# Attention values with queries on partitions: the turned P becomes the stationary operand, V the moving one, and the softmax factor is applied to x

## The chip, the cores and the metric

The kernel runs on one core of one Trainium2 chip. The metric is the device time in microseconds (us) of one execution of the whole program; lower is better. A core has five engines that run their own instruction streams side by side: TensorE (PE, with its weight loads shown apart as PEld), VectorE (DVE), ScalarE (ACT), GpSimd (POOL) and SyncE (SP, which here only issues DMA). Each stream is in program order, and semaphores tie them together.

## The reference

Two stages. First a windowed attention with a linear position bias over 8 batches, 8 heads, 576 positions and a head width of 64; a query sees itself and the 127 positions before it:

```python
scores = scale * (q @ k.T) + slope[h] * -(i - j)     # kept where 0 <= i - j < 128
attn = exp(scores - rowmax); attn /= attn.sum(-1) + 1e-9
x = (attn @ v)                                       # then (B, H, S, D) -> (4608, 512)
```

Then a "soft" mixture of experts over all 4608 tokens with 32 slots, 4 for each of 8 experts:

```python
logits = x @ phi                                     # 4608 x 32
d = softmax over tokens (axis 0); slot_input = d.T @ x
slot_out[e] = relu(slot_input[e] @ w1[e]) @ w2[e]    # 512 -> 1024 -> 512
c = softmax over slots (axis 1);  out = c @ slot_out
```

All arithmetic is float32.

## The kernel before, in words

**Tiles and groups.** A batch has 576 = 4 x 128 + 64 queries, so five query tiles t = 0 to 4, the last one (the tail) 64 wide. A group (b, t, g) is four heads of a full tile (g = 0 or 1), or all eight heads of a tail, two heads side by side in the 128 partitions. That makes 72 groups. One turn of the main loop (lines 770 to 797) handles several groups at different stages; each engine executes its share in the order written, since the whole kernel is scheduled by hand (`manual_schedule`).

**One group on its way.** `scores` (L227) puts the position bias (bf16, L248, or L236 for t = 0) and q k^T (L255, or L241) into one of two PSUM tiles `s4`, for t > 0 as 32-query strips with a key window of 160. On DVE, `merge` folds the window to 128 columns (L268, L270, L272), `rowmax` reduces it (L290) and `bias` scales the maximum (L293). On ACT, `expo` writes P = exp(...) of four heads to SBUF and sums its rows (L342). POOL adds the epsilon (`total`, L298), DVE inverts (L302), and `normalise` multiplies each of the four 128 x 128 blocks of P by its row's factor on DVE (L307). Three turns later PE transposes the four blocks (`flip`, L352), ACT copies them out of PSUM (`split`, L359), and POOL masks them into the part that belongs to the same key tile, `pd`, and the one that belongs to the key tile before, `pp` (L361, L363, for tails L366, L368). One turn after that, `values` multiplies:

```python
for ph in halves_of:                    # previous and own key tile
    for par in range(2):                # head of the pair -> PSUM partitions 0-63 or 64-127
        nc.tensor.matmul(
            xp[D * par:D * par + D, j, 0:w],
            lhsT=v_slot[b, t - 1 + ph][0:rows, D * h:D * h + D],     # stationary: V, 64 columns
            rhs=src[:, 2 * par + i] ...,                             # moving: P^T, 128 columns
            start=(ph == halves_of[0]), stop=(ph == halves_of[-1]))
```

(L388.) x comes out transposed, 128 feature rows of two heads by w queries. One such float32 matmul is two instructions in the trace, each with its own weight load. A group of t = 1 to 3 has 16 such loads and matmuls, one of t = 0 has 8 (no key tile before it), a tail has 32.

**After the values of a tile.** ACT copies x from PSUM (`x_store`, L404), PE transposes it back to tokens on partitions (`x_flip`, L409) and ACT copies that (`x_keep`, L418), because the mixture needs x both ways round: for the logits (`logits`, L427) and for the slot inputs (`slot_sum`, L510). The mixture's online softmax over tokens runs once for each batch, over the four full tiles as four "lanes" of 32 rows; the tails of two batches share a tile, which is handled behind every odd batch by further, narrow steps (`logits_tail` L438, small flips L468 and L496, `slot_tail` L517). The last batch is in the order 1, 2, 3, 4, 0 and has its own closing code (lines 799 to 880): two lanes, then a join with three more.

**The rest.** The main loop puts its PE work in the order flip, values, scores of the next group, then what `todo` holds under "pe" (x_flip, logits and so on). DMA is issued by SP in program order: q three groups ahead, K and V as their slots come free, and expert weights, 64 units of 512 KB, of which 36 go into a ring during attention and 11 into places (`place`) that attention has left. After attention come `hidden` (L911, first expert layer), `expert_out` (L947), `slot_stack` (L960), `slot_inputs` before it (L661, the only place besides `slot_stack` where a full 128 x 128 float32 block that isn't being transposed is the stationary operand), and `combine` (L968, L974, output DMA L976).

Of the kernel before, what the change touches and what calls it, by code (L numbers as in the profile page):

```python
# [10 lines left out]
F32 = mybir.dt.float32  # L11
# [10 lines left out]
DM = H * D  # L22
# [20 lines left out]
EAGER = 2  # L43
FLAG = 3
LAG = 4
FINAL = (3, 4, 0)
# [8 lines left out]


def width(t):
    return P if t < 4 else TAIL
# [10 lines left out]
def tile_attn_softmoe(  # L69
# [26 lines left out]
    fine = cpool.tile([P, 14], F32, name="fine")  # L96
    low, m_run, s_run = fine[:, 0:1], fine[:, 1:3], fine[:, 3:4]
    comb = cpool.tile([P, NS], F32, name="comb")
    mix = cpool.tile([P, NS], F32, name="mix")
# [7 lines left out]
    area = cpool.tile([P, 19, HW], F32, name="area")  # L107

    kall = kq[:, 0:NB * P].rearrange("p (n j w) -> p n j w", n=NB, j=NPAIR)
    qs = [kq[:, NB * P + 2 * P * i:NB * P + 2 * P * i + 2 * P] for i in range(3)]  # L110
    half = [slice(64 * par, 64 * par + 64) for par in range(2)]

    def halves(i):
        return area[:, i].rearrange("p (u w) -> p u w", u=4)

    xts = [halves(i) for i in (0, 1, 12, 13)]
    xt_t = halves(17)
    p4s = [halves(i) for i in (2, 3, 18)]
    pas, pps = [halves(i) for i in (6, 8, 7)], [halves(i) for i in (7, 9)]
    vs = [area[:, i] for i in (11, 5, 10)]  # L120
    xns = [area[:, i] for i in (16, 4, 14, 15)]
# [3 lines left out]
    areas = {i: area[:, i:i + 2].rearrange("p a w -> p (a w)") for i in range(0, 18, 2)}  # L125
    place = [ks[1], areas[14], ks[0], ks[2]] + [areas[i] for i in (0, 10, 6, 4, 16, 12, 8)]
# [16 lines left out]
    def order(b):  # L143
        return (1, 2, 3, 4, 0) if b == last else range(NT)

    def pos(b, t):
        return order(b).index(t)

    def lane(b, t):
        return (t - 1) % 4 if b == last else t  # L150

    groups = [(b, t, g) for b in range(B) for t in order(b) for g in range(2 if t < 4 else 1)]
    number = {key: i for i, key in enumerate(groups)}
    n = len(groups)
    v_loads = [(b, t) for b in range(B) for t in range(NT)]
    fin = slice(3 * NS, P)
# [7 lines left out]
    def load_q(i, eng=None):  # L164
        b, t, g = groups[i]
        o = 4 * P * t + 2 * P * g
        (eng or nc.sync).dma_start(qs[i % 3], qd[b, :, o:o + 2 * P])
# [4 lines left out]

    v_slot = {}

    def load_v(again=False):
        if again:
            b, t, v_slot[last, 0] = last, 0, area[:, 13]
        else:
            b, t = v_loads[len(v_taken)]
            v_slot[b, t] = vs[len(v_taken) % 3]  # L180
            v_taken.append((b, t))
        nc.sync.dma_start(v_slot[b, t][0:width(t)], vd[b, P * t:P * t + width(t)])

    def load_v_pair():
        new = [len(v_taken), len(v_taken) + 1]
        for i in new:
            v_slot[v_loads[i]] = vs[i % 3]
            v_taken.append(v_loads[i])
        for o in (0, DM // 2):
            for i in new:  # L190
                b, t = v_loads[i]
                nc.sync.dma_start(
                    v_slot[b, t][:, o:o + DM // 2], vd[b, P * t:P * t + P, o:o + DM // 2])
# [3 lines left out]
    with tc.manual_schedule(engines=ORDERED):  # L197
        warm = area[:, 2].bitcast(BF16)[:, 0:512]
# [4 lines left out]
        nc.vector.memset(fine[:, 10:11], -1.0)  # L203
# [11 lines left out]
        for i in range(WARM):  # L215
            nc.tensor.matmul(free[i % 4], lhsT=warm[:, 0:P], rhs=warm, start=True, stop=True)
        nc.gpsimd.memset(lg, LOW)
        nc.gpsimd.memset(area[:, 3, 0:P], 1.0)
        nc.gpsimd.affine_select(
            unit_r, area[:, 3, 0:P], [[1, P]], ALU.is_equal, 0.0, base=0, channel_multiplier=-1)  # L220
        load_v()
        nc.scalar.dma_start(cst[:, P:], cstd)
        nc.scalar.dma_start(phi, phid)
        for t in range(2, NT):
            load_k(0, t)

    def scores(i):  # L227
        b, t, g = groups[i]
        s4 = s4s[i % 2]
# [867 lines left out]
```

## Time and profile before

| | us |
|---|---|
| three runs | 290.46, 290.97, 292.67; median 290.97 |
| span of the profiled execution (first to last instruction) | 289.1 |
| median of the runs less that span | 1.9 |
| first merge on DVE to last merge (attention loop) | 5.4 to 219.1 |
| last merge to the first matmul of `hidden` | 219.1 to 235.7 |
| `hidden` to the end | 235.7 to 289.1 |

In the profile, a row of a timeline reads: start in us, length in us, engine, line, operation, output<-inputs, shape, xcount, and in brackets the idle time ahead with what ended it. In a shape, "128*64 128x64" means an array tile of 128 rows by 64 columns and operands of 128 partitions by 64 elements. For a weight load the second number of the array tile is the number of columns that are loaded. In the list of groups the number behind the bar is busy time in us, the mean of one in ns, then the engine's idle time ahead of the group and what ended most of it.

### The profile page before, as it was taken

What the parts mean: (1) busy time and instruction counts of PE and PEld (TensorE: products, weight loads), DVE (VectorE), ACT (ScalarE), POOL (GpSimd) and SP (SyncE); (2) the same over time, 40 slices, a digit from 0 to 9 for tenths busy, and PEclk for the clock granted to TensorE, in tenths of its full rate; (3) what the DMA queues carried; (4) which work ended last, traced back from release to release, by engine and by line L of the source; (5) the groups of instructions that cost most, each with busy time, mean ns of one, the idle gap of its engine ahead of it and who ended that gap; (6) DMA issues with size and microseconds to landing.
All of it is one profiled execution on the core that took longest, in us unless ns stands there. A gap on an engine that the chain in (4) does not pass through costs nothing.

```text
span 289.1 us, 13085 instructions
## 1 busy us (share of the span) xinstructions
PE 272.9 (94%) x5164; PEld 191.0 (66%) x5164; DVE 233.3 (81%) x729; ACT 204.5 (71%) x811; POOL 92.7 (32%) x206
## 2 busy tenths in 40 slices
PE   7499999999999999999999999999899999999983
PEld 3367777777677767776777677767676753476641
DVE  3899999999989999988999999979989443234452
ACT  2788888978988978978798887978797241023351
POOL 2025515442444354235324550634455001000000
PEclk9799999999999999999999999999999999999995
DMA  6645278868786887867678869675547789999897
GB/s 193 223 131 169 81 228 266 261 201 284 212 265 201 287 279 242 246 231 247 216 249 258 282 199 291 218 252 173 185 158 238 231 285 311 417 417 398 352 378 285
DMA packets 35025, 72.58 MB, mean 251 GB/s; under 512 B 4210, under 2 KB 15124, under 8 KB 34964
## 3 DMA queue, kind: packets, MB, share of 16 engines
q1 hardware_dynamic: 34244, 71.24, 74.0%
q8 instruction: 41, 0.67, 0.9%
q10 hardware_dynamic: 720, 0.51, 0.6%
q14 instruction: 20, 0.16, 0.1%
HBM read 62.29 MB, written 9.44 MB: 248 GB/s over the span
## 4 chain that ended last, share of the span: by engine, by line
PE 47%; DVE 44%; ACT 3%; issue 3%; POOL 1%; ACTq 0%; DVEq 0%; POOLq 0%
DVE area L307 16%; DVE s L290 11%; PE xp L388 8%; DVE s L270 6%; PE op L947 5%; PE hp L911 5%; PE po L968 4%; PE pt L352 4%; PE s L255 4%; DVE s L268 3%; PE xq L409 2%; PE lp L427 2%; ACT area L342 2%; PE s L248 2%; PE ap L510 1%
## 5 line engine op out<-in xcount | busy, mean ns | idle before, releaser
L342 ACT ACTIVATE area<-s,nb 128x128 f32<-128x128 f32 x288 | 102.5, 374 | 21.5 <-DVE nb L293 20.2
L307 DVE TENSOR_SCALAR area<-area,rs 128x128 f32<-128x128 f32 x286 | 79.2, 338 | 0.6 <-DVE nb L293 0.3
L388 PE MATMUL xp<-area 128*64 128x128 f32 (+1 forms) x1104 | 75.2, 271 | 2.2 <-POOL area L361 1.3
L388 PEld LDWEIGHTS xp<-area 128*64 128x64 f32 x1104 | 56.2, 136 | 17.4 <-issue 8.7
L342 ACT ACTIVATION_READ_ACCUMULATOR area<-s,nb 128x1 f32 x288 | 60.8, 211 | 0.0
L290 DVE TENSOR_REDUCE s<-s 128x4 f32<-128x512 f32 x71 | 49.5, 698 | 2.2
L359 ACT COPY area<-pt 128x512 f32<-128x512 f32 x70 | 42.0, 600 | 11.0 <-PE pt L352 10.8
L298 POOL TENSOR_SCALAR rs<-sm 128x4 f32<-128x4 f32 x70 | 13.8, 197 | 99.7 <-ACT area L342 98.9
L352 PE MATMUL pt<-unit_r,area 128*128 128x128 f32 x284 | 45.6, 282 | 0.0
L255 PE MATMUL s<-kq 64*32 64x160 f32 x1792 | 42.0, 302 | 0.3 <-DMA kq<-k_t 0.3
L352 PEld LDWEIGHTS pt<-unit_r,area 128*128 128x128 f32 x284 | 31.9, 142 | 14.2 <-PE s L255 5.0
L361 POOL TENSOR_SCALAR_AFFINE_SELECT area<-area 128x512 f32<-128x512 f32 x48 | 31.6, 658 | 25.8 <-ACT area L359 24.5
L270 DVE COPY_PREDICATED s<-cst,s 128x512 f32<-128x512 int32 x48 | 32.9, 686 | 0.7 <-PE s L255 0.5
L363 POOL TENSOR_SCALAR_AFFINE_SELECT area<-area 128x512 f32<-128x512 f32 x48 | 31.4, 655 | 3.3
L255 PEld LDWEIGHTS s<-kq 64*32 64x32 f32 x1792 | 29.6, 107 | 1.0 <-DMA kq<-q_t 0.5
L248 PE MATMUL s<-ramp,ones 64*32 64x320 bf16 x448 | 18.7, 310 | 5.0 <-ACT area L342 4.8
L974 DVE COPY ob<-po 128x384 f32<-128x384 f32 x24 | 12.5, 554 | 13.5 <-PE po L968 11.8
L409 PE MATMUL xq<-unit_r,area 128*128 128x128 f32 x136 | 22.0, 284 | 0.5
L404 ACT COPY area<-xp 128x512 f32<-128x512 f32 (+1 forms) x37 | 20.9, 565 | 2.0 <-PE xp L388 1.6
L418 ACT COPY area<-xq 128x512 f32<-128x512 f32 x34 | 20.8, 611 | 0.0
L974 ACT COPY ob<-po 128x384 f32<-128x384 f32 x24 | 10.5, 482 | 13.7 <-PE po L968 13.7
L409 PEld LDWEIGHTS xq<-unit_r,area 128*128 128x128 f32 x136 | 14.5, 141 | 6.4 <-issue 3.2
(167 smaller groups left out, 309.8 us busy)
## 6 DMA issues: line engine op xcount, KB each, us to landing
w<-w SPq DMA_DIRECT2D x53, 512.0 KB, 5.1
out<-ob SPq DMA_DIRECT2D x24, 384.0 KB, 4.2
kq<-q_t SPq DMA_DIRECT2D x69, 128.0 KB, 3.2
kq<-k_t SPq DMA_DIRECT2D x32, 256.0 KB, 3.7
area<-v_n SPq DMA_DIRECT2D x31, 256.0 KB, 4.3
area<-w SPq DMA_DIRECT2D x8, 512.0 KB, 5.0
area<-v_n SPq DMA_DIRECT2D x12, 128.0 KB, 3.4
kq<-w SPq DMA_DIRECT2D x3, 512.0 KB, 6.3
```

The costliest lines, as they stand in the source:

```text
L248: nc.tensor.matmul(s4[32 * c:32 * c + 32, 2 * par:2 * par + 2, 32 * r:32 * r + WIN], lhsT=ones[rows, 0:32], rhs=ramp[rows, h], start=True, ...
L255: nc.tensor.matmul(s4[32 * c:32 * c + 32, 2 * par + jj, 32 * r:32 * r + WIN], lhsT=qt[rows, 2 * h + jj if t == 4 else jj, 32 * r:32 * r + 32],
L270: nc.vector.copy_predicated(s4[:, :, P:2 * P], bc(mask_u, 1, 4), s4[:, :, 0:P])
L290: nc.vector.tensor_reduce(st[key]["mx"][:, us], merged(key, us), axis=AX.X, op=ALU.max, negate=True)
L307: mul(p4[:, u], p4[:, u], st[key]["rs"][:, u:u + 1])
L342: nc.scalar.activation(s["p4"][:, u], merged(key, u), AF.Exp, bias=s["nb"][:, u:u + 1], scale=SCALE, accum_out=s["sm"][:, u:u + 1],)
L352: nc.tensor.transpose(s["pt"][:, u], s["p4"][:, u], ident)
L359: copy(pa[:, us], s["pt"][:, us])
L361: nc.gpsimd.affine_select(pp[:, us], pa[:, us], [[0, m], [-1, P]], ALU.is_gt, 0.0, base=0, channel_multiplier=1)
L363: nc.gpsimd.affine_select(pa[:, us], pa[:, us], [[0, m], [1, P]], ALU.is_ge, 0.0, base=0, channel_multiplier=-1)
L388: nc.tensor.matmul(xp[D * par:D * par + D, j, 0:w], lhsT=v_slot[b, t - 1 + ph][0:rows, D * h:D * h + D], rhs=src[:, 2 * par + i] if t < 4 ...
L409: nc.tensor.transpose(xq[:, P * j:P * j + P], x_of(b, t)[:, j], ident)
```

## The change

- `values`: P^T is the stationary operand (all 128 queries as columns, lines `pp`, `pd`), V moves, 64 columns for a head, and x comes out with queries on partitions. The counts stay 16 (t = 1 to 3) and 8 (t = 0) loads and matmuls a group.
- The tails of an even batch and the next odd one form one tile of 128 queries, which is handled with the odd batch in two groups like any other; its matmuls take 64 columns of P^T at a time and go to PSUM partitions 0-63 and 64-127. The key tile of the tail is padded with zeros to 128 rows (`v4_even`, `v4_odd`), so that both parts use all 128 rows. There are still 72 groups, now 36 tiles of two.
- `normalise` is gone. `x_store` on DVE multiplies x on its way out of PSUM by the factor of its query and head, one 128 x 512 instruction for a tile. `total` (POOL) and `inverse` (DVE) run once for a tile rather than once for a group.
- `x_store` gives the token layout, so `x_flip` makes the transposed one; `x_keep` copies that. Their number is 36, one for each tile. `x_flip` stands ahead of `flip` in the next turn.
- The mixture handles nine sets of four tiles, all alike; the narrow steps for tails and the join of the last batch are gone. The last set is in the closing code, with three lanes and then the fourth.
- P is turned two turns after its scores rather than three (`FLAG`), and its values come after three rather than four (`LAG`).
- SBUF: V in four slots rather than three, extra slots for the tails' K and V, six rows of x rather than four, 15 places for early weights rather than 11. On the host, q is laid out anew. The call that builds the program gets `dynamic_dma_scratch_size=64`.

The core of the diff:

```diff
-FLAG = 3
-LAG = 4
+FLAG = 2
+LAG = 3
+NXN = 6
+NQ = NTT // 4
...
-    place = [ks[1], areas[14], ks[0], ks[2]] + [areas[i] for i in (0, 10, 6, 4, 16, 12, 8)]
+    place = [ks[1], ks[0], ks[2]] + [areas[i] for i in (0, 14, 2, 4, 10, 8, 12, 6, 20, 22, 16, 18)]
...
-        return (1, 2, 3, 4, 0) if b == last else range(NT)
...
-    groups = [(b, t, g) for b in range(B) for t in order(b) for g in range(2 if t < 4 else 1)]
+        return (1, 2, 3, 4, 0) if b == last else range(4 + b % 2)
+
+    tiles = [(b, t) for b in range(B) for t in order(b)]
+    groups = [(b, t, g) for b, t in tiles for g in range(2)]
...
+    def load_k_even(b):
+        nc.sync.dma_start(kt, kd[b, :, 3 * 4 * P:NB * P])
...
+    def load_v_tails(b):
+        nc.sync.dma_start(v3_even, vd[b, 3 * P:4 * P])
+        nc.sync.dma_start(v4_even[0:TAIL], vd[b, 4 * P:S])
+        nc.sync.dma_start(v4_odd[0:TAIL], vd[b + 1, 4 * P:S])
...
-    def normalise(key, us, mul=nc.vector.tensor_scalar_mul):
-        p4 = st[key]["p4"]
-        for u in range(4)[us]:
-            mul(p4[:, u], p4[:, u], st[key]["rs"][:, u:u + 1])
+    def total(k):
+        st["rs", k] = work.tile([P, H], F32, tag="rs", name="rs")
+        nc.gpsimd.tensor_scalar(st["rs", k], st.pop(("sm", k)), EPS, 1.0, op0=ALU.add, op1=ALU.mult)
+
+    def inverse(k):
+        nc.vector.reciprocal(st["rs", k], st["rs", k])
...
+    def softmax_front(i):
+        new = groups[i]
         merge(new)
+        rowmax(new, ALL)
+        bias(new, ALL)
         filler()
         filler()
+        if i % 2 and i > 1:
+            inverse((i - 3) // 2)
...
+        for jj in range(2):
+            for par in range(2):
+                u, h = 2 * par + jj, 4 * g + 2 * jj + par
+                cols = slice(D * h, D * h + D)
+                for ph in (1,) if t == 0 else (0, 1):
+                    src = (pp, pd)[ph][:, u]
+                    if t < 4:
+                        nc.tensor.matmul(
+                            xp[:, cols], lhsT=src, rhs=v_slot[b, t - 1 + ph][:, cols],
+                            start=(ph == 0 or t == 0), stop=(ph == 1))
+                    else:
+                        for rows, v in zip(half, ((v3_even, v_slot[b, 3]), (v4_even, v4_odd))[ph]):
+                            nc.tensor.matmul(
+                                xp[rows, cols], lhsT=src[:, rows], rhs=v[:, cols],
+                                start=(ph == 0), stop=(ph == 1))
+
+    def x_store(k, hs=slice(0, H)):
+        cols = slice(D * hs.start, D * hs.stop)
+        nc.vector.tensor_tensor(
+            xns[k % NXN][:, cols].rearrange("p (h d) -> p h d", d=D),
+            st["x", k][:, cols].rearrange("p (h d) -> p h d", d=D),
+            bc(st["rs", k][:, hs], 2, D), op=ALU.mult)
...
+        x_store(k)
+        do("flip", i + 1, x_flip, k)
+        do("act", i + 1, x_keep, k)
+        if k % 4 == 3:
+            do("pe", i + 1, logits, q)
...
-                softmax_front(new, groups[i - 1])
+                softmax_front(i)
...
+            if i and i % 2 == 0:
+                total(i // 2 - 1)
+            run("flip", i)
             if i >= FLAG:
                 flip(groups[i - FLAG])
                 split(groups[i - FLAG])
             run("act", i)
             if i >= LAG:
                 values(groups[i - LAG])
-                after_values(i, groups[i - LAG])
             if i + 1 < n:
                 scores(i + 1)
+            if i >= LAG:
+                after_values(i, groups[i - LAG])
...
-    nc = bacc.Bacc("TRN2", target_bir_lowering=False, num_devices=1)
+    nc = bacc.Bacc("TRN2", target_bir_lowering=False, num_devices=1, dynamic_dma_scratch_size=64)
```

More of the change, by code (lines that the diff above doesn't have):

```diff
@@ new lines, in x_store, with x_flip @@
+    def x_store(k, hs=slice(0, H)):
[4 more added lines that the diff above has]
+            bc(st["rs", k][:, hs], 2, D), op=ALU.mult)
+    def x_flip(k, to=None, js=range(NPAIR)):
+        if ("xq", k) not in st:
+            st["xq", k] = ps_1.tile([P, DM], F32, tag="xq", name="xq") if to is None else to
+        for j in js:
+            nc.tensor.transpose(st["xq", k][:, P * j:P * j + P], xns[k % NXN][:, P * j:P * j + P], ident)
@@ L471, in token_exp, with slot_flip @@
[L471 to L474 removed]
+        nc.vector.tensor_scalar_mul(nm, mn, -1.0)
+        st["n", q] = nm
+    def slot_flip(q, src=None):
+        if ("d", q) not in st:
+            st["d", q] = ps_1.tile([P, 512], F32, tag="mi", name="dp")
+        st["c", q] = st["d", q][:, 2 * P:3 * P]
+        nc.tensor.transpose(st["c", q], lg[:, 0:P] if src is None else src, ident)
+    def token_exp(q, src=None):
+        odd = q % 2
+        nm = st.pop(("n", q))
@@ L506, in slot_sum, with token_flip, token_keep @@
-    def slot_sum(b):
-        dn = st["d", b]
-        ap = ps_1.tile([P, DM], F32, tag="mi" if b < last else "pt", name="ap")
-        for c in range(lanes(b)):
+    def token_flip(q):
+        if ("d", q) not in st:
+            st["d", q] = ps_1.tile([P, 512], F32, tag="mi", name="dp")
+        nc.tensor.transpose(st["d", q][:, 0:P], lg[:, 0:P], ident)
+    def token_keep(q, copy=nc.scalar.copy):
+        dn = work.tile([P, P], F32, tag="dn", name="dn", bufs=1)
+        copy(dn, st["d", q][:, 0:P])
+        st["dn", q] = dn
@@ L510, in slot_sum @@
+    def slot_sum(q, to=None):
+        dn = st["dn", q]
+        ap = ps_1.tile([P, DM], F32, tag="mi" if to is None else to, name="ap")
+        for c in range(4):
             nc.tensor.matmul(
-                ap[NS * c:NS * c + NS], lhsT=dn[:, NS * c:NS * c + NS], rhs=xns[c],
-                start=True, stop=(c < 3 or not with_tail(b)),
-            )
-        st["a", b] = ap
-    def slot_tail(b):
-        nc.tensor.matmul(st["a", b][fin], lhsT=st["d", b][:, P:], rhs=xn_of(b, 4), start=False, stop=True)
@@ L600, in join @@
-    def join():
-        st["join"] = ps_1.tile([P, 512], F32, tag="pt", name="join")
-        nc.tensor.matmul(st["join"][fin], lhsT=comb, rhs=acc, start=True, stop=True)
-    def join_keep():
-        nc.scalar.copy(sums[fin], st["join"][fin])
-    lf = free[2]
-    sums = area[:, 3]
-    def logits_last(c):
-        src = x_of(last, FINAL[c])
-        for j in range(NPAIR):
-            nc.tensor.matmul(
-                lf[fin, P * c:P * c + P], lhsT=phi[:, j], rhs=src[:, j], start=(j == 0), stop=(j == NPAIR - 1))
```

654 lines of the change are left out of this document (230 added, 424 removed).

## The prediction, made blind

> **What bounds the kernel now.** I read the page's engine table first, then the busy times by stretch: most of the attention loop (20 to 205 us) and the experts (236 to 278). A row of the second has the stretch, its length, the busy us of PE, PEld, DVE, ACT and POOL, the granted clock, the DMA share and GB/s.
>
> ```profile
> span 289.1 us, 13085 instructions
> ...
> PE 272.9 (94%) x5164; PEld 191.0 (66%) x5164; DVE 233.3 (81%) x729; ACT 204.5 (71%) x811; POOL 92.7 (32%) x206
> ```
>
> ```profile
> 20.00:205.00 185.00, 182.73 (x3731) 134.72 (x3732) 176.18 (x556) 159.12 (x656) 77.58 (x166) 1.00 0.74 233
> 236.00:278.00 42.00, 41.90 (x742) 23.40 (x734) 15.69 (x44) 9.61 (x24) 0.96 (x3) 1.00 0.96 370
> ```
>
> In the loop PE is busy 182.7 of 185 us and DVE 176.2; the granted clock is 1.00. Two engines are full at once. The chain of waits, which can name only one, names DVE there:
>
> ```profile
> 149.73 0.62 DVE s L270
> ...
> 150.37 0.70 DVE s L290
> ...
> 151.25 0.87 DVE area L307 x4
> 152.12 0.61 DVE s L270
> ```
>
> A plain group takes 152.12 - 149.73 = 2.39 us, of which L307, the step that the change removes, has 0.87. Whether its removal pays is decided by PE. Its weight loads, in order, over one turn:
>
> ```profile
> 98.98 0.14 PEld L466 LDWEIGHTS dp<-unit_r,lg 128*128 128x128 f32 x1 [0.25 <-issue]
> 99.04 0.47 PEld L352 LDWEIGHTS pt<-unit_r,area 128*128 128x128 f32 x4
> 99.68 0.85 PEld L388 LDWEIGHTS xp<-area 128*64 128x64 f32 x16 [0.17 <-issue]
> 100.70 0.11 PEld L248 LDWEIGHTS <-ones 64*32 64x32 bf16 x8 [0.17 <-DVE nm L456]
> 100.73 0.53 PEld L255 LDWEIGHTS s<-kq 64*32 64x32 f32 x32
> 101.50 0.14 PEld L494 LDWEIGHTS dp<-unit_r,lg 128*128 128x128 f32 x1 [0.25 <-ACT al L480]
> 101.56 0.47 PEld L409 LDWEIGHTS xq<-unit_r,area 128*128 128x128 f32 x4
> 102.00 0.47 PEld L352 LDWEIGHTS pt<-unit_r,area 128*128 128x128 f32 x4
> 102.64 0.20 PEld L388 LDWEIGHTS xp<-area 128*64 128x64 f32 x4 [0.17 <-issue]
> ```
>
> From start to next start: values 100.70 - 99.68 = 1.02 us; scores 101.50 - 100.70 = 0.80; an x_flip 102.00 - 101.56 = 0.44; a flip 102.64 - 102.00 = 0.64. A plain group with flip, values and scores needs 0.64 + 1.02 + 0.80 = 2.46 us of PE, as much as DVE's 2.39. So relief for DVE alone buys next to nothing, and whatever values cost more is paid in full.
>
> **Part 1, values.** The new stationary block has 128 columns where the old one had 64. The trace has one stage of just that form, L661: full 128 x 128 float32 blocks, not transposed, and even fewer moving columns, 32.
>
> ```profile
> 234.72 0.52 PEld L661 LDWEIGHTS s<-mix,area 128*128 128x128 f32 x4
> 234.75 0.60 PE L661 MATMUL s<-mix,area 128*128 128x32 f32 x4
> 235.16 0.53 PEld L661 LDWEIGHTS bank<-mix,area 128*128 128x128 f32 x4
> 235.74 0.11 PEld L911 LDWEIGHTS hp<-w,acc 128*32 128x32 f32 x1
> 91.75 0.31 PEld L388 LDWEIGHTS xp<-area 128*64 128x64 f32 x8
> 125.25 0.42 PEld L388 LDWEIGHTS xp<-area 128*64 128x64 f32 x8 [0.17 <-issue]
> 125.83 0.11 PEld L248 LDWEIGHTS <-ones 64*32 64x32 bf16 x8 [0.17 <-issue]
> ```
>
> Four such loads take 235.16 - 234.72 = 0.44, so 0.110 us each; eight with the way out to the next stage 235.74 - 234.72 = 1.02. The old loads of 64 columns come in pairs, one for each half of the array. With 64 moving columns (91.75, eight in 0.31, the last one's own 0.14 off, so three steps of 0.17) a pair costs about 0.057. The step goes with the loaded columns, 0.11 for 128 and 0.057 for 64, and a full block leaves no other half to share it. Moving 64 columns instead of 128 then gains nothing: the load is the longer part.
>
> New values for t = 1 to 3: 1.02 + 8 x 0.110 = 1.90, against 1.02: +0.88 in 48 groups = +42.2. For t = 0: 1.02 against 125.83 - 125.25 = 0.58: +0.44 in 16 groups = +7.0. Together **+49.3** (896 loads at 0.055 more); by the rounding of the step, 47 to 51.5.
>
> [...]
>
> **Part 2, the way into values.** A flip followed by values takes 0.64, four transposes followed by four of the same array tile 0.44. I read the 0.20 as the price of changing the array tile from 128*128 to 128*64. The new values stay on 128*128: 64 x 0.20 = **-12.8**. No row shows a transpose followed by a plain full-block matmul; bounds 0 and 64 x 0.25 (the longest bracket above) = -16.
>
> **Part 3, tails.** The old tail has 32 loads in mixed forms:
>
> ```profile
> 90.94 0.23 PEld L388 LDWEIGHTS xp<-area 128*64 128x64 f32 x4 [0.25 <-issue]
> 91.37 1.34 PEld L388 LDWEIGHTS xp<-area 64*64 64x64 f32 x28 [0.21 <-POOL area L368]
> 92.78 0.11 PEld L248 LDWEIGHTS <-ones 64*32 64x32 bf16 x8
> ```
>
> 92.78 - 90.94 = 1.84. The new one has 32 loads as well, all 128*64 thanks to the zero rows: 16 pairs x 0.057 + 0.17 = 1.08. Eight groups x -0.76 = **-6.1**; bounds 0 (the cost is not the change between 64 and 128 rows) and -6.1.
>
> **Part 4, the mixture.** Behind each of three odd batches `logits_tail` (L438) and `slot_tail` (L517) go; one more set of four lanes moves into the loop.
>
> ```profile
> L427 PE MATMUL lp<-area,phi 128*32 128x128 f32 x240 | 9.0, 276 | 0.1
> L510 PE MATMUL ap<-area,dn 128*32 128x512 f32 x60 | 8.5, 605 | 0.0
> L517 PE MATMUL ap<-area,dn 128*32 128x512 f32 x6 | 3.1, 605 | 0.0
> L438 PE MATMUL lp<-area,phi 128*32 128x128 f32 x24 | 3.1, 273 | 0.0
> L466 PE MATMUL dp<-unit_r,lg 128*128 128x128 f32 x7 | 2.3, 328 | 0.0
> L248 PE MATMUL s<-ramp,ones 64*32 64x320 bf16 x448 | 18.7, 310 | 5.0 <-ACT area L342 4.8
> L307 DVE TENSOR_SCALAR area<-area,rs 128x128 f32<-128x128 f32 x286 | 79.2, 338 | 0.6 <-DVE nb L293 0.3
> L523 DVE SCALAR_TENSOR_TENSOR acc<-acc,al,ap 128x512 f32<-128x512 f32 x6 | 4.5, 742 | 4.1 <-PE ap L517 4.1
> ```
>
> Off: 3.1 + 3.1 = 6.2. On: 32/240 of 9.0 + 8/60 of 8.5 + two flips of 0.33 = 3.0. Net **-3.2**; bounds -6 and 0.
>
> **Part 5, waits of today.** PE is truly idle 4.8 us ahead of scores, for `expo` to free a score bank. With turns of about 3 us ACT (204.5 busy in all, x_store included, which goes to DVE) is never last: **-4.8**; bounds 0 and -6.4 (with the other small waits).
>
> **Part 6, x_store ahead of x_flip.** `x_store` on DVE starts when values end, and takes about 0.74 (nearest row L523, also 512 columns from PSUM). PE meanwhile does the scores, 0.80, and then wants x_flip. With some 0.14 (about one load's length, an estimate) until the last value is out, 0.08 is missing: 36 x 0.08 = **+3**; bounds 0 and, with DVE late by 0.4, +14. What waits behind x_flip on PE is the flip and so everything. This cover is gone where no scores follow (closing code).
>
> **At nothing.** DVE loses 79 us of L307 and gains 36 x 0.74 = 27; with 233 - 79 + 27 = 181 us over the run it hides behind PE, which needs about 239 for the loop, as do ACT and POOL (totals and masks). The extra K and V loads go through SP's queue, where q is issued three groups ahead, and turns get longer. The shorter lag moves `flip` and `values` one turn up, the same distance apart. For the smaller DMA scratch no row shows a cost.
>
> Loop: 49.3 - 12.8 - 6.1 - 3.2 - 4.8 + 3 = **+25.4**. Between these two merges, the first and the last of the loop, 213.7 us become 239:
>
> ```profile
> 5.39 0.43 DVE L268 COPY_PREDICATED s<-cst,fine 128x256 f32<-128x256 int32 x1 [3.69 <-issue]
> ...
> 219.14 0.69 DVE L268 COPY_PREDICATED s<-cst,fine 128x512 f32<-128x512 int32 x1
> ```
>
> **Part 7, the end.** The experts keep PE full (41.90 of 42) and do not change. Then output DMA decides:
>
> ```profile
> 278.58 0.96 PE po L968 x8
> ...
> 280.05 4.27 PE po L968 x14
> ```
>
> 14 at 0.12 would be 1.7, so 2.6 us wait for output buffers. Fifteen units come early instead of 11, 2.1 MB less beside the outputs: **-2.5**; bounds -6 (also a shorter closing chain without the join) and +2.
>
> **Sum.** Profiled span 289.1 + 25.4 - 2.5 = 312.0; the median of the runs lies 291.0 - 289.1 = 1.9 above it: **314 us**.
>
> **Rivals.** *Wide loads are hidden* (the other side). If a wide load costs no more than the 0.055 of today, Part 1 is nothing and the other parts stand: 314 - 49 = 265 us. For it: today's loads vanish behind their matmuls altogether, and the transposes load 128 columns with no cost that shows. Against it: L661, where nothing else can fill 0.110. Without Part 1 the rest comes to 22.9 - 49.3 = -26.4 us, or 0.029 for each of 896 loads; so it decides from a load under 0.055 + 0.029 = 0.084. Chance 0.06.
>
> *Loads and matmuls add up.* Each full-block load waits for the matmul before it, 0.057 for 64 columns: 314 + 896 x 0.057 = 365 us. The L661 step speaks against it (0.110, where 0.138 would stand); for it, that these are eight instructions only. 0.03.
>
> *x_store late.* In turns with mixture work DVE has up to 2 us more ahead of it, x_flip then waits half a microsecond a tile: 36 x 0.5 = 18, less the 3 counted: 329 us. For it: one bank for x, x_flip right behind. Against: DVE is then idle for over a third of the loop. 0.11.
>
> *The savings cancel the loads.* All parts at their favourable bounds are 289.1 + 47 - 16 - 6.1 - 6 - 6.4 - 6 = 295.6 with nothing for Part 6, 297.5 with the 1.9; if the way out of values gets shorter too, as a tail's is in the rows of Part 3 (from the end of its loads, 92.71, to 92.78: 0.07 instead of 0.17; 64 x 0.10 = 6.4), it ends at 291, no change. 0.05, of which 0.02 for a little faster still.
>
> **How the numbers follow.** The forecast has 0.75. The range runs from the favourable bounds taken together, 297, to 332, which takes in the x_store rival and 18 us of the unfavourable bounds; outside lie the first two rivals, most of the last and the far ends. A measurement of this kernel can tell about 1% from no change. Faster by over 1%: 0.06 + 0.02 = 0.08. Within 1%: 0.05 - 0.02 = 0.03. Slower: 0.75 + 0.03 + 0.11, 0.89.
>
> **What would show it.** Right: loads of the values line are 128*128, sixteen take about 1.75 us from first start to last end, and the chain names PE throughout the loop, DVE idle by a third. Part 2: sixteen loads begin without the 0.17 bracket after a flip. Part 3: a tail's 32 loads all 128*64, about 1.1 us. Part 6: brackets of 0.1 at x_flip. Wrong: wide loads closer than 0.08, or PE with waits of more than a few tenths a turn on DVE.

## The result, and the profile after

The changed kernel takes 322.44 us (median of four runs, 321.33 to 324.43) beside 290.74 us for the kernel before on the same chip; the ratio is 1.1095 [1.1037, 1.1153], so it is slower by 11%. The forecast was 314 in a range of 297 to 332. The profiled execution took 324.43 us (span 322.7). Medians here and below are of all runs of a kernel, while the ratios leave out those over 1.5% above its fastest.

From the page of the kernel after, the span, the engine table, the granted clock in 40 slices, and the chain that ended last, by engine and by line:

```profile
span 322.7 us, 12515 instructions
...
PE 305.7 (95%) x5143; PEld 241.8 (75%) x5143; DVE 181.8 (56%) x443; ACT 187.5 (58%) x769; POOL 85.3 (26%) x162
...
PEclk9659999999999999999999999999999975999998
...
PE 88%; DVE 6%; issue 2%; ACT 1%; POOL 1%; DVEq 0%; ACTq 0%; POOLq 0%
PE xp L362 29%; PE pt L327 10%; PE s L247 9%; PE xq L382 6%; PE hp L734 6%; PE op L770 5%; PE s L236 4%; PE po L791 4%; PE ap L449 3%; PE lp L392 3%; PE xp L367 2%; PE s L229 2%; DVE area L373 1%; DVE s L282 1%; PE dp L414 1%
```

DVE lost 51 us of work and is down to 6% of the chain, where it had 44%; PE carries 88% of it, and the new values line, L362, 29% of the span alone. The busy times by stretch (columns as for the kernel before) say the same of the loop:

```profile
10.10:23.70 13.60, 12.50 (x158) 10.29 (x157) 6.46 (x15) 7.89 (x36) 1.78 (x5) 0.50 0.60 189
...
20.00:205.00 185.00, 183.38 (x3295) 158.77 (x3279) 120.66 (x286) 130.73 (x554) 62.30 (x112) 0.99 0.68 215
...
262.00:273.00 11.00, 10.02 (x45) 3.62 (x45) 2.12 (x10) 0.00 (x0) 0.00 (x0) 0.53 0.68 239
```

Between 20 and 205 us PE is busy for 183.4 of 185 us and DVE for only 120.7. The first and the third row show something that I had not priced: in two stretches the granted clock is about half. Ahead of the first PE stood still, with `expo` on ACT not done (a row of PE's timeline):

```profile
11.20 0.47 PE L236 MATMUL s<-ramp,ones 64*32 64x320 bf16 x8 [1.92 <-ACT area L317]
```

The weight loads of some turns, in order:

```profile
100.30 1.86 PEld L362 LDWEIGHTS xp<-area 128*128 128x128 f32 x16
102.24 0.11 PEld L236 LDWEIGHTS <-ones 64*32 64x32 bf16 x8
...
103.54 0.47 PEld L327 LDWEIGHTS pt<-unit_r,area 128*128 128x128 f32 x4
103.97 0.97 PEld L362 LDWEIGHTS xp<-area 128*128 128x128 f32 x8
105.01 0.11 PEld L236 LDWEIGHTS <-ones 64*32 64x32 bf16 x8
...
115.96 0.42 PEld L382 LDWEIGHTS xq<-unit_r,area 128*128 128x128 f32 x4 [0.30 <-DVE area L373]
...
246.88 0.42 PEld L382 LDWEIGHTS xq<-unit_r,area 128*128 128x128 f32 x4 [0.84 <-DVE area L373]
...
247.91 1.01 PEld L367 LDWEIGHTS xp<-area 128*64 128x64 f32 x32 [0.17 <-issue]
248.99 0.42 PEld L327 LDWEIGHTS pt<-unit_r,area 128*128 128x128 f32 x4
```

From start to next start: values of t > 0 take 102.24 - 100.30 = 1.94 us (forecast 1.90), of t = 0 105.01 - 103.97 = 1.04 (1.02), the way from a flip into values 103.97 - 103.54 = 0.43 and without a bracket (0.44), a tail 248.99 - 247.91 = 1.08 (1.08). A tail is back on half-width loads, and there the 0.17 bracket is back too.

**Where the time lies.** The loop's first, 17th and last merge on DVE mark its start, the end of its first 16 groups, and its end; for the kernel before, the 17th is quoted here first, then the two first ones of the kernel after (its last stands at 247.69).

```profile
45.68 0.69 DVE L270 COPY_PREDICATED s<-cst,s 128x512 f32<-128x512 int32 x1
```

```profile
5.91 0.43 DVE L260 COPY_PREDICATED s<-cst,fine 128x256 f32<-128x256 int32 x1 [4.22 <-issue]
...
56.84 0.69 DVE L262 COPY_PREDICATED s<-cst,s 128x512 f32<-128x512 int32 x1
```

In the same way from the other traces, in us (closing: last merge to the first matmul of `hidden`; hidden: from there to the first of `expert_out`; end: the rest of the span; the kernels are those of the next section):

| profiled execution | groups 1 to 16 | groups 17 to 72 | closing | hidden | end | span |
|---|---|---|---|---|---|---|
| before | 40.3 | 173.5 | 16.6 | 15.3 | 38.1 | 289.1 |
| after | 50.9 | 190.9 | 16.5 | 20.8 | 37.8 | 322.7 |
| half loads | 39.7 | 175.6 | 15.6 | 20.7 | 37.6 | 295.3 |
| PE kept busy | 46.5 | 190.8 | 16.5 | 17.7 | 38.7 | 315.5 |
| busy in the closing code alone | 47.1 | 190.8 | 18.0 | 17.7 | 37.8 | 317.6 |
| x_flip behind flip | 44.9 | 188.5 | 16.9 | 19.4 | 37.5 | 312.8 |
| eleven early units | 48.9 | 190.8 | 16.0 | 19.7 | 37.8 | 318.7 |
| half loads, x_flip | 40.4 | 173.9 | 15.2 | 20.7 | 37.6 | 293.8 |
| half loads, x_flip, busy | 40.3 | 171.1 | 15.2 | 17.7 | 38.9 | 289.1 |
| the same, weights spread evenly | 42.2 | 168.3 | 15.2 | 17.7 | 38.9 | 288.2 |

After against before: the first 16 groups +10.6, the other 56 +17.4, closing -0.1, hidden +5.5, the end -0.3.

**Theory after the result.** The wide loads of `values` carry the loop, as forecast; the 10.7 us by which the span exceeds the forecast span of 312.0 come mostly from the halved clock at the start and in `hidden`, and from an end that didn't get shorter. **Rivals:** that full-block `values` cost by something other than the width of the load (order, stalls); that x_flip's waits are a large part; that `hidden` waits for weights rather than for the clock.

### The profile page after: what moved, and what is told of

Its sections match the earlier page's. It is cut to its first block, busy times and chain, and to the rows that moved or that the text cites. A ratio compares the mean times of both kernels' runs of the same rounds, so it can differ in the third digit from the quotient of the medians.

```text
span 322.7 us, 12515 instructions
## 1 busy us (share of the span) xinstructions
PE 305.7 (95%) x5143; PEld 241.8 (75%) x5143; DVE 181.8 (56%) x443; ACT 187.5 (58%) x769; POOL 85.3 (26%) x162
## 4 chain that ended last, share of the span: by engine, by line
PE 88%; DVE 6%; issue 2%; ACT 1%; POOL 1%; DVEq 0%; ACTq 0%; POOLq 0%
PE xp L362 29%; PE pt L327 10%; PE s L247 9%; PE xq L382 6%; PE hp L734 6%; PE op L770 5%; PE s L236 4%; PE po L791 4%; PE ap L449 3%; PE lp L392 3%; PE xp L367 2%; PE s L229 2%; DVE area L373 1%; DVE s L282 1%; PE dp L414 1%
## 5 line engine op out<-in xcount | busy, mean ns | idle before, releaser
L362 PE MATMUL xp<-area 128*128 128x64 f32 x880 | 107.2, 275 | 0.0
L362 PEld LDWEIGHTS xp<-area 128*128 128x128 f32 x880 | 105.5, 195 | 0.0
L336 POOL TENSOR_SCALAR_AFFINE_SELECT area<-area 128x512 f32<-128x512 f32 x48 | 30.6, 637 | 76.2 <-ACT area L334 75.9
L327 PEld LDWEIGHTS pt<-unit_r,area 128*128 128x128 f32 x284 | 32.9, 144 | 7.8 <-issue 5.2
L373 DVE TENSOR_TENSOR area<-xp,rs 128x512 f32<-128x512 f32 x35 | 24.1, 689 | 19.4 <-PE xp L362 16.2
L338 POOL TENSOR_SCALAR_AFFINE_SELECT area<-area 128x512 f32<-128x512 f32 x48 | 30.7, 639 | 3.3
L289 POOL TENSOR_SCALAR rs<-sm 128x8 f32<-128x8 f32 x36 | 10.1, 280 | 74.0 <-ACT area L317 59.0
L382 PEld LDWEIGHTS xq<-unit_r,area 128*128 128x128 f32 x140 | 15.2, 143 | 14.2 <-DVE area L373 11.1
L382 PE MATMUL xq<-unit_r,area 128*128 128x128 f32 x140 | 23.1, 288 | 1.8 <-DVE area L373 1.4
L734 PE MATMUL hp<-w,inp 128*8 128x512 f32 (+1 forms) x128 | 18.6, 690 | 0.4 <-DVE inp L534 0.4
L260 DVE COPY_PREDICATED s<-cst,fine 128x512 f32<-128x512 int32 (+1 forms) x17 | 11.3, 664 | 11.9 <-PE s L229 7.6
```

The lines of the kernel that those rows point to most:

```text
L327: nc.tensor.transpose(s["pt"][:, u], s["p4"][:, u], ident)
L336: nc.gpsimd.affine_select(pp[:, us], pa[:, us], [[0, m], [-1, P]], ALU.is_gt, 0.0, base=0, channel_multiplier=1)
L338: nc.gpsimd.affine_select(pa[:, us], pa[:, us], [[0, m], [1, P]], ALU.is_ge, 0.0, base=0, channel_multiplier=-1)
L362: nc.tensor.matmul(xp[:, cols], lhsT=src, rhs=v_slot[b, t - 1 + ph][:, cols], start=(ph == 0 or t == 0), stop=(ph == 1))
L382: nc.tensor.transpose(st["xq", k][:, P * j:P * j + P], xns[k % NXN][:, P * j:P * j + P], ident)
L734: nc.tensor.matmul(hp[nb][NS * c:NS * c + w], lhsT=inp[:, o:o + w], rhs=wt[0, 4 * g + c, 2 * nb + kk][:, 512 * kp:512 * kp + 512], start=( ...
```

## The experiments

**Half loads.** The kernel after, with each full-block matmul of `values` cut into two over the query halves: 32 loads of 64 columns instead of 16 of 128, the same product.

```diff
-                        nc.tensor.matmul(
-                            xp[:, cols], lhsT=src, rhs=v_slot[b, t - 1 + ph][:, cols],
-                            start=(ph == 0 or t == 0), stop=(ph == 1))
+                        for rows in half:
+                            nc.tensor.matmul(
+                                xp[rows, cols], lhsT=src[:, rows], rhs=v_slot[b, t - 1 + ph][:, cols],
+                                start=(ph == 0 or t == 0), stop=(ph == 1))
```

> The changed kernel, with each full-tile value matmul split into two over the query halves: the stationary block is 128 rows by 64 queries, twice as many loads and matmuls (32 for t = 1 to 3), the same sum of columns loaded and twice the columns moved. Theory (a 128-column load sets the step of 0.11 us; two 64-column loads for the two halves of the array run side by side at 0.057 a pair): sixteen columns-pairs take about 0.95 us and values with their way in about 1.25 instead of 1.94, since the way in costs its 0.2 again. 48 groups x -0.66 and 16 x -0.22 is -35 us: about 287 us. Rival (the time is in the wait of x_flip for x_store, or in the lower clock): 316 us or more.

Measured: 296.86 us (four runs, 292.23 to 299.59, too far apart for a ratio). Its weight loads:

```profile
103.33 0.47 PEld L327 LDWEIGHTS pt<-unit_r,area 128*128 128x128 f32 x4
103.96 1.01 PEld L363 LDWEIGHTS xp<-area 128*64 128x64 f32 x32 [0.17 <-issue]
105.04 0.11 PEld L236 LDWEIGHTS <-ones 64*32 64x32 bf16 x8
```

Twice as many loads take 105.04 - 103.96 = 1.08 us instead of 1.94, and the change of array tile costs 103.96 - 103.33 = 0.63 instead of 0.43: Parts 1 and 2 each seen alone. The loop from the 17th group falls from 190.9 to 175.6, so the width of the load is the main price. The total missed the expected 287 by 10 us. (`hidden` still took 20.7, at a granted clock of 0.50 from 235.2 to 245.5 us, but so it did in the kernel after, from which the 287 was reckoned.) Between 20 and 205 us PE now had pauses of 9.7 us in all: 3.3 for x_store, 1.4 for `expo`, 0.4 for a DMA, and 4.6 that the profile puts down to nothing; these are taken up below.

**x_flip behind flip.** The kernel after, with x_flip issued behind the flip of its turn, so that DVE's x_store has a flip's time more.

```diff
-            run("flip", i)
             if i >= FLAG:
                 flip(groups[i - FLAG])
+            run("flip", i)
+            if i >= FLAG:
                 split(groups[i - FLAG])
```

> The changed kernel, with x_flip behind the flip of the same turn instead of ahead of it, so that x_store has 0.6 us more. Theory (x_flip's wait for x_store costs about a tenth of a microsecond a tile): 2 to 4 us less, 318.5 to 320.5 us, and no wait for the store is left at x_flip. Rival (x_store's lateness is a main part of the loss, up to the 11 us that x_flip's loads sat idle on it): 8 to 12 us less.

Measured: 317.22 us (314.51 to 322.56), ratio 1.09 [1.0869, 1.093]. The group rows of x_flip's loads, first of the kernel after, then of this one (last column: idle time ahead, and what ended it):

```profile
L382 PEld LDWEIGHTS xq<-unit_r,area 128*128 128x128 f32 x140 | 15.2, 143 | 14.2 <-DVE area L373 11.1
```

```profile
L382 PEld LDWEIGHTS xq<-unit_r,area 128*128 128x128 f32 x140 | 16.3, 141 | 0.8 <-DVE area L373 0.8
```

The wait for x_store is all but gone, and the loop from the 17th group is 2.4 us shorter (190.9 to 188.5), as my theory expected and not 8 to 12: of the 14.2 us of idle weight loading most lay beside running matmuls (PE itself waited 1.4 us for x_store there). The median fell by 5.2 us, past the expected 2 to 4 (317.22, not 318.5 to 320.5). In the profiled executions, which lie 9.9 us apart, 6.0 of it are in the first 16 groups, where this one has the clock in full (1.00 from 6 to 50 us; 44.9 us, not 50.9), and 1.4 in `hidden`.

**PE kept busy.** The kernel after, with extra bf16 matmuls whose result nobody reads, put where PE waited: 17 in the first five turns, 20 in the closing code.

```diff
+    def busy(to, k):
+        rhs = ramp.rearrange("p a b w -> p (a b w)")[:, 0:512]
+        for _ in range(k):
+            nc.tensor.matmul(to, lhsT=ones, rhs=rhs, start=True, stop=True)
...
+            if i < 5:
+                busy(idle, (0, 3, 8, 4, 2)[i])
...
+        busy(free[0], 2)
         x_flip(kb, free[2], range(0, 2))
         x_flip(kb, js=range(2, 4))
+        busy(free[0], 4)
...
```

> The changed kernel, with TensorE kept busy by extra bf16 matmuls, whose results nobody reads, where it sat idle: 17 of them in the first turns of the loop and 20 in the closing code. Theory (the granted clock fell to a half from 10 to 24 us and from 263 to 273 us because TensorE sat idle just before, and it cost about half of that time where TensorE sets the pace): both stretches are granted full clock, the expert layer's first stage takes 15.5 us again instead of 21, and the whole is 7 to 10 us shorter: about 313 to 315 us. Rival (the clock falls for another reason, as the kind of work, or the time is bound by DMA there): the clock rows stay as they are and the time within 2 us of 322.

Measured: 317.67 us (317.19 to 319.12), ratio 1.0938 [1.0913, 1.0964]; the clock is full (1.00) until 311.1 us, in the last outputs. More matmuls, and less time by 322.44 - 317.67 = 4.8 us. By stage: the first 16 groups 50.9 to 46.5, hidden 20.8 to 17.7. It is less than the 7 to 10 that I expected. To see the closing code alone, the same without the first 17:

> The changed kernel with the extra matmuls in the closing code alone. Theory (the halved clock in the experts' first stage comes of TensorE's idle time in the closing code and costs there what e2 got back): the clock is full between 255 and 275 us, the experts' first stage takes 17 to 18 us instead of 20.8, the whole 319 to 320 us; the first turns keep their halved clock in some executions, so that single times spread over 5 us as the changed kernel's. Rival (the gain of e2 was in the first turns): 322 us, within 1 us of the changed kernel.

Measured: 319.11 us (317.05 to 319.64), ratio 1.0954 [1.0915, 1.0992]; the total and `hidden` (17.7) are as expected. In the profiled execution `hidden` is 3.1 us shorter than in the kernel after and the closing code 1.5 longer; another 3.8 us are in the first 16 groups, which this edit doesn't touch. What remains of `hidden` is seen in its PE rows (L549 are the extra matmuls), beside those of the kernel after, and of before:

```profile
262.05 1.04 PE L746 MATMUL hp<-w,inp 128*32 128x512 f32 x2 [0.35 <-DVE inp L534]
263.02 0.61 PE L549 MATMUL s<-ramp,ones 128*128 128x512 bf16 x2
263.47 0.53 PE L528 MATMUL s<-comb,acc 128*128 128x32 f32 x4
263.93 1.06 PE L746 MATMUL hp<-w,inp 128*32 128x512 f32 x8
264.92 0.61 PE L549 MATMUL s<-ramp,ones 128*128 128x512 bf16 x2
265.45 0.22 PE L514 MATMUL lanes<-fine,comb 128*32 128x1 f32 x2
265.61 0.33 PE L414 MATMUL dp<-unit_r,lg 128*128 128x128 f32 x1
265.86 9.62 PE L746 MATMUL hp<-w,inp 128*8 128x512 f32 x86
```

```profile
257.87 1.06 PE L392 MATMUL s<-area,phi 128*32 128x128 f32 x8 [0.92 <-DVE area L385]
259.60 0.27 PE L499 MATMUL lanes<-unit_r,fine 128*1 128x128 f32 x1 [0.67 <-DVE fine L405]
260.25 0.33 PE L438 MATMUL dp<-unit_r,lg 128*128 128x128 f32 x1 [0.38 <-ACT lg L420]
...
264.15 1.92 PE L734 MATMUL hp<-w,inp 128*32 128x512 f32 x2 [0.35 <-DVE inp L534]
265.99 1.06 PE L528 MATMUL s<-comb,acc 128*128 128x32 f32 x4
...
267.59 13.11 PE L734 MATMUL hp<-w,inp 128*32 128x512 f32 x94
280.63 0.38 PE L521 MATMUL dp<-fine,cst 32*128 32x1 f32 x2
```

```profile
235.74 7.16 PE L911 MATMUL hp<-w,acc 128*32 128x512 f32 x64
242.83 0.37 PE L677 MATMUL dp<-unit_r,lg 32*128 32x32 f32 x3
```

Before, 64 matmuls took 242.83 - 235.74 = 7.09 us, 0.111 each, and nothing else stood among them. After, 94 took 280.63 - 267.59 = 13.04, which at 0.111 would be 10.4: half the clock (0.50) until 272.9. The rows ahead of `hidden` in the kernel after show what precedes it: PE waits 0.92, 0.67 and 0.38 us for DVE and ACT, one step after another; filled with matmuls, these waits don't halve the clock for so long (3.4 us, from 251.4 to 254.8, in this kernel). In the kernel with extra matmuls the stretch is 17.7, of which they have (263.47 - 263.02) + (265.45 - 264.92) = 0.98; so the clock costs about 20.8 - 16.7 = 4.1 of the 5.5 us. The second half of `slot_inputs` (263.93 - 263.47 = 0.46) and two small steps (265.86 - 265.45 = 0.41) now stand inside `hidden`; before, they did not. That is 0.9 of the other 1.4.

**Eleven early units.** The kernel after with 11 early places for expert weights instead of 15.

```diff
-    place = [...] + [areas[i] for i in (0, 14, 2, 4, 10, 8, 12, 6, 20, 22, 16, 18)]
+    place = [...] + [areas[i] for i in (0, 14, 2, 4, 10, 8, 12, 6)]
```

> The changed kernel with 11 places for early weights instead of 15, as before the change; the four units come later through the ring. The prediction's last part (four units early take 2.5 us off the end): 2.5 us longer than the changed kernel, about 325 us. Rival (TensorE and the copies of the last outputs set the end, DMA has slack since the experts' first stage was slow): within 1 us of it, 322 us; the stretch from the first output matmul of the experts to the end stays at 37.8 us give or take 0.5.

Measured: 323.11 us (320.43 to 324.27), ratio 1.1098 [1.1048, 1.1147]: no difference, and the stretch from `expert_out` to the end is 37.8 us in both. `hidden` doesn't wait for weights either: with four units fewer early it takes 19.7 us, not more than 20.8. The last 16 matmuls of `combine`, first in the kernel after, then here:

```profile
313.98 3.11 PE L791 MATMUL po<-ln,slot 32*128 32x384 f32 x16 [0.53 <-ACT ob L797]
```

```profile
309.95 3.17 PE L787 MATMUL po<-ln,slot 32*128 32x384 f32 x16 [0.53 <-ACT ob L793]
```

Three microseconds, with or without the four units; what the end waits for is not the weights beside it.

**DVE's relief alone.** The kernel before, without the 288 multiplications of `normalise`; this leaves out the division of the softmax.

```diff
     def normalise(key, us, mul=nc.vector.tensor_scalar_mul):
         p4 = st[key]["p4"]
-        for u in range(4)[us]:
-            mul(p4[:, u], p4[:, u], st[key]["rs"][:, u:u + 1])
+        return
```

> The kernel before, with its 288 normalising multiplications (L307) left out, so that P goes on without its factors; nothing else is changed. Theory (TensorE was as full as VectorE, 2.46 against 2.39 us a plain group): the loop loses its waits and the stretched turns only, 3 to 9 us: 282 to 288 us, VectorE idle over a quarter of the loop. Rival (VectorE alone was the bound, as the chain of waits has it with 16% of the span in L307): 250 us or less.

Measured: 286.61 us, ratio 0.9861 [0.9838, 0.9885]. Between 20 and 205 us:

```profile
20.00:205.00 185.00, 183.65 (x3821) 136.33 (x3820) 118.23 (x315) 161.60 (x667) 77.94 (x170) 1.00 0.75 236
```

DVE falls from 176.2 to 118.2 us and PE rises by less than one, to 183.65. All that the change could win by relief of DVE is 4 us.

**Half loads with both other edits.** Half loads and x_flip behind flip; then the extra matmuls as well. The diffs are those above.

> The split of the value matmuls and x_flip behind the flip, without the extra matmuls. Theory: with TensorE no longer held by wide loads, x_flip's wait for x_store (its loads sat idle on it for 14.5 us with the split alone) counts in full: the loop from the seventeenth group on 167 to 170 us, against 175.6 with the split alone; the experts' first stage keeps its halved clock, about 20 us; the whole 287 to 291 us. Rival: no more than 1 us of difference to the split alone in that loop.

> Three edits on the changed kernel together: value matmuls split over the query halves (64-column loads), x_flip behind the flip of the same turn, and the extra matmuls that keep TensorE busy in the first turns and in the closing code. Theory (loads of 128 columns, the wait for x_store and the halved clock are what the change lost by): the loop from the seventeenth group on falls from 176 us with the split alone to about 168, the experts' first stage from 20.7 to 16 to 18 us, the whole to 283 to 287 us, below the kernel before. Rival (with the loads narrow, q and K loads that wait in SP's queue set the loop): the loop stays at 174 us or more, the whole at 290 us or more.

Measured: 291.33 us (287.02 to 295.5), ratio 0.9961 [0.9923, 0.9999], and with the extra matmuls 290.47 (285.82 to 298.2), 0.9922 [0.9884, 0.996]. So 31.1 of the 31.7 us of the loss are gone (322.44 - 291.33; 322.44 - 290.74). But both kernels fell short: the first one's loop takes 173.9 us where 167 to 170 were expected, the second one's 171.1 instead of 168, its whole 290.47 instead of 283 to 287, and its single times spread over 12 us. The waits of PE between 20 and 205 us (line, releaser, us in all, times, longest) name something that neither the kernel before nor after has:

```profile
PE s L247 <- issue: 2.3, 4, 1.1
PE pt L327 <- issue: 1.1, 1, 1.1
PE xp L363 <- issue: 0.8, 2, 0.5
PE s L236 <- ACT area L317: 0.7, 2, 0.4
PE xp L368 <- issue: 0.3, 1, 0.3
PE lp L393 <- issue: 0.2, 1, 0.2
```

The rows with "issue", a wait that this view puts down to nothing, come to 4.7 us, and one of 1.1 lies between two transposes of the same flip. The table of DMA queues has a queue of instructions, 40 packets in the kernel after, 48 here:

```profile
q8 instruction: 40, 0.66, 0.8%
```

```profile
q8 instruction: 48, 0.79, 1.1%
```

One packet is 0.66 MB / 40 = 16 KB. New theory: with 6076 PE matmuls instead of 5143 PE outruns the arrival of its own instructions, whose packets the table counts to the same 16 DMA engines as the data (1.1% of their time, beside 75.7% for the data's q1). Three kernels test it, all from the last one: no expert weights during the loop (36 units issued three groups before its end, so the total says nothing); 16 tiny matmuls more for each group of t > 0; and the units of the loop cut in halves of 64 partitions.

```diff
-        if i >= W0 and loaded[0] < NW and (NW - loaded[0]) * (WEND - W0 - 2) >= NW * (WEND - i):
-            load_weight()
         if i == n - 3:
+            for _ in range(NW):
+                load_weight()
```

> The split loads with x_flip behind flip and the extra matmuls, but the 36 expert units that were loaded during the loop are all issued three groups before its end, so that the hidden stage waits for them; only the loop is to be read, not the total. In the earlier run of this kernel with the weights in the loop, the loop from the 17th to the last merge took 171.1 us instead of the expected 168, and the stretch 20 to 205 us held 9 pauses of PE longer than 0.25 us, 4.96 us in all, most of them with no releaser that the profile shows, several right after a 16 KB block of instructions began to arrive. Theory: PE then waits for its next instructions, whose fetch is slowed by the other transfers; without the 18.9 MB of weights in the loop the pauses fall below 1.5 us and the loop to 166 to 168. Rival: the pauses come from the rate at which instructions are fetched, whatever else moves, or from something not tied to transfers: the pauses stay at 4 to 8 us and the loop at 170 to 172.

```diff
+            for _ in range(2):
+                for par, rows in enumerate(half):
+                    for c in range(4):
+                        nc.tensor.matmul(
+                            s4[32 * c:32 * c + 32, 2 * par, 0:2],
+                            lhsT=ones[rows, 0:32], rhs=ramp[rows, 0, 0, 0:2], start=True, stop=True)
```

> The split loads with x_flip behind flip and the extra matmuls, and 16 further tiny matmuls (2 moving columns, overwritten afterwards) ahead of the scores of each group of t > 0: 2048 more PE instructions counting the loads. Their own time is estimated at 0.2 to 0.3 us a group, 10 to 15 us of loop. Theory (PE waits for its next instructions): the pauses of PE over 0.25 us in 20 to 205 us, 4.96 us before, at least double. Rival (pauses not tied to instructions): they stay between 3 and 7 us. The total time says nothing here.

```diff
-WEND = 66
-W0 = 10
+WEND = 69
+W0 = 3
...
+        rows = half[part]
+        nc.sync.dma_start(wt[unit][rows], (w1d, w2d)[m][e, rows, UW * k:UW * (k + 1)])
```

> The split loads with x_flip behind flip and the extra matmuls, and the 36 expert units of the loop issued in halves of 64 partitions, about one half a turn, from turn 4 to turn 69 instead of 11 to 66: the same bytes, spread more evenly. Theory (instruction blocks arrive late when large transfers stand in front of them): the pauses of PE over 0.25 us in 20 to 205 us fall from 4.96 us to 1 to 3 us, the loop from 171.1 to 166 to 169, the time to 285 to 288 us. Rival (the mean load of the DMA engines decides, not how it is cut): pauses of 3 to 6 us, loop 169 to 172, time 288 to 292 us.

Measured between 20 and 205 us (one execution each of the first two), first without weights in the loop, then with more instructions, then with half units:

```profile
20.00:205.00 185.00, 183.95 (x4781) 145.85 (x4774) 140.18 (x339) 153.42 (x658) 73.90 (x137) 1.00 0.52 154
```

```profile
20.00:205.00 185.00, 172.55 (x4926) 135.25 (x4927) 124.25 (x297) 136.33 (x581) 63.69 (x119) 0.99 0.75 229
```

```profile
20.00:205.00 185.00, 172.19 (x4286) 133.69 (x4270) 126.55 (x305) 138.76 (x594) 65.58 (x122) 0.98 0.91 229
```

| kernel | DMA share | PE pauses over 0.25 us, in all | of these without a releaser | groups 17 to 72 |
|---|---|---|---|---|
| half loads, x_flip, busy | 0.78 | 4.96 | 4.31 | 171.1 |
| no weights in the loop | 0.52 | 0.98 | 0 | 161.9 |
| more instructions | 0.75 | 11.54 | 10.50 | 186.5 |
| half units | 0.91 | 12.36 | 10.37 | 180.8 |

(The tiny matmuls are 56 x 16 = 896, so 1792 instructions with their loads, not the 2048 of the expectation.) All pauses without a releaser go when the weights go (PE is busy for 183.95 of 185 us, and the loop is 9 us shorter), and they more than double when instructions are added at the same DMA load. So both sides of the theory hold. The loop without weights is shorter than the 166 to 168 expected: it fell by 9 us and the pauses by 4, and where the other 5 lie isn't shown.

The records of the single transfers tie the pauses to the blocks. Before the pause of 1.1 us inside the flip, a packet of q8 started at 157.93 us and landed at 158.86 (the table of DMA queues for 157.5 to 158.5 us, then PE's row behind the pause):

```profile
q8 instruction: 1, 0.02, 5.8%
```

```profile
160.24 0.49 PE L327 MATMUL pt<-unit_r,area 128*128 128x128 f32 x3 [1.13 <-issue]
```

So PE goes on 160.24 - 158.86 = 1.38 us after the landing. In four kernels with such pauses (half loads with x_flip and busy, more instructions, half units, and the evenly spread weights of the next experiment) all 30 of them over 0.25 us end 0.97 to 1.70 us after a packet of q8 landed, though there are only 48 of these packets in the 289.1 us of the first of them, one every 6 us. Of the causes considered, only late instructions would put the end of every pause there.

The half units were meant as the cure and were the opposite: cut over partitions, the same bytes kept the DMA engines busy for 0.91 of the time (0.77 with whole units over the same turns, in the next experiment), the pauses rose as the theory then has it, and the time was 302.29 us, ratio 1.0409 [1.0357, 1.0461].

**Weights spread evenly.** Whole units again, over turns 4 to 69 (`W0 = 3`, `WEND = 69`).

> The split loads with x_flip behind flip and the extra matmuls, and the 36 whole expert units of the loop spread over turns 4 to 69 instead of 11 to 66 (not cut, since the cut ones kept the DMA engines busy for 0.91 of the loop instead of 0.78). Pauses of PE over 0.25 us in 20 to 205 us so far: 0.98 us at a DMA share of 0.52, 4.96 at 0.78, 12.36 at 0.91. Theory: with fewer weights per turn (36 in 65 turns for 36 in 55) the share falls to about 0.75 and the pauses to 3 to 4.5 us, the loop to 168 to 171, the time to 286 to 290 us. Rival: no difference from the 290.47 us of the uneven spread, since single blocks of instructions are late whatever the mean: 289 to 292 us.

Measured: 287.44 us (283.76 to 289.94), ratio 0.9848 [0.9801, 0.9895]: the one version with the whole computation that is faster than the kernel before by over 1%. In its profiled execution (289.94 us) the DMA share is 0.77 and the loop from the 17th group is down to 168.3, but the first 16 groups are up by 1.9 and the pauses are as long as before the edit (4.92 us, not 3 to 4.5). Time and loop are in the expected range. That the evener spread itself helps is likely but not settled: the interval of its ratio still touches that of the uneven spread (0.9922 [0.9884, 0.996]), and its shorter pauses aren't seen.

## Why the prediction was right or wrong

- **Bound and sign: right.** PE bounds the loop, relief of DVE alone is worth 4 us (286.61), and values cost more PE time than it can win.
- **Part 1, +49.3: right.** 1.94 and 1.04 us where 1.90 and 1.02 stood (48 x 0.92 + 16 x 0.46 = 51.5, its upper bound), and undone by half loads (1.08). Of the rivals, "wide loads hidden" and "loads and matmuls add up" fall by the same rows: 15 steps within 1.86 us, the last load's own 0.14 off, are 0.115 each, not 0.055 and not 0.110 + 0.057 = 0.167. (The 0.138 at L661 in the second of them is worked out the same way, 0.110 and half of 0.057, for 32 moving columns. That a load waits for the matmul before it, no run shows.)
- **Part 2, -12.8, and Part 3, -6.1: right** (0.43; 1.08). The bracket comes back exactly where the array tile changes (half loads, tails).
- **Part 4, -3.2: larger.** On PE's rows from each start to the next, between the first and the last merge, the mixture's steps without x_flip take 24.1 us before and 18.8 in the kernel with PE kept busy: -5.3, within the bounds.
- **Part 5, -4.8: three of it.** PE's idle time ahead of the scores' bias fell from 5.0 to 2.0 us (1.92 of it at once, at the start's half clock).
- **Part 6, +3: right in size.** Moving x_flip back gives 2.4. But there is no 0.08 at each of 36 tiles: PE's own waits for x_store between 20 and 205 us are three, 1.2 us in all, the longest 0.7.
- **The loop, +25.4.** With the clock full (PE kept busy) groups 1 to 72 take 46.5 + 190.8 = 237.3 us, so +23.6. The profiled kernel has +28.0, because its start runs at half clock for 13.6 us: 50.9 - 46.5 = 4.4. That 23.6 comes so near to 25.4 is partly luck. Counted as for Part 4, flip and values grew by 29.1 (Parts 1 to 3 have 30.4) and the mixture saved 2.1 more than forecast. Scores and x_flip together saved 3.5 (Parts 5 and 6 have 1.8), while the extra matmuls, which stand in for waits, add 3.7.
- **The step that failed: Part 7, "The experts keep PE full and do not change", end -2.5.** `hidden` took 5.5 us more. PE is busy there all the same, but at half the granted clock until 272.9, after a closing code with many short waits, and it took over work from the closing code. The end gained 0.3, and the four additional early units are worth nothing. The error was to price `hidden` by its work at full clock, and to take the wait for output buffers for one that fewer bytes beside it would shorten.
- **The sum.** 312.0 + 4.4 (start's clock) + 5.5 (hidden) + 2.2 (end) + 0.5 (the first merge is at 5.9, not 5.4) - 1.8 (loop at full clock) - 0.1 (closing) = 322.7. The rival with 329, x_store late by 18 us, lies nearer to 322 than the forecast does, but not by its mechanism: moving x_flip back was worth 2.4 us in the loop, not 18.
- **Still open:** why the clock at the start stayed low for 13.6 us though PE worked, half a microsecond in `hidden`, and 5 of the 9 us that the loop lost with its weight transfers.

## What to carry to other kernels

When operands swap roles, price the loads and not only the matmuls: the count stayed 16 here, and the time nearly doubled. On a PE that is full, a float32 load of 128 columns cost 0.11 us here where two of 64, one for each half of the array, cost 0.057 together, though they load as many columns for the same product. Two further prices are missed by a sum of durations: short waits ahead of a stage halved the clock inside it here (4.1 us in `hidden`), and more, smaller instructions made PE wait for their arrival (4.3 us of pauses). Read the granted clock and the "issue" waits before the group table.

## What the runs showed of the hardware that was not expected

**The granted clock.** The half-clock stretches ahead of the last outputs lasted 3.4 us (11.5 to 14.9, before), 6.8 and 6.8 (eleven early units), 10.2 (262.7 to 272.9, after) and 13.6 (10.1 to 23.7, after): one, two, three and four times 3.4 us; why in such steps, no run shows. As far as the profile's busy time is what counts, steady work did not end the longest one soon: in 10.1 to 23.7 PE was busy for 12.5 of 13.6 us, without a break from 11.2 on, at a granted clock of 0.50. Nor did a longer idle time give a longer dip: the kernel before stood still for 4.1 us ahead of 11.3 and had 3.4 us of half clock, the kernel after stood still for 1.9 and had 13.6. How much of a run is at half clock changes between executions of one program: the six runs of x_flip behind flip have mean granted clocks from 0.954 to 0.981 and take 322.56 to 314.51 us.

**Instructions arrive late.** The pauses named "issue" (those over 0.25 us, between 20 and 205 us) grew with the DMA share, from 0 at a share of 0.52 over 4.31 at 0.78 to 10.37 at 0.91, and with the number of PE instructions, to 10.50 with 1792 more at 0.75. The q8 rows have packets of 16 KB; with 6076 matmuls on PE in 290 us, 4.31 us of 185 were such pauses. The link rests on the three kernels and on the landings of the blocks, 0.97 to 1.70 us ahead of the end of each of these pauses; the profile itself names no block as the releaser of a wait.
